# Later loads issued by SyncE instead of GpSimd, twelve closing steps on GpSimd, and a bf16 product at the end

## The chip, the cores and the metric

The kernel runs on one core of one Trainium2 chip. The metric is the device time of one execution in microseconds (us); less is better. A core has five engines with a queue of instructions each: PE (TensorE, matmuls), DVE (VectorE), ACT (ScalarE), POOL (GpSimd) and SP (SyncE, which here only issues transfers). Within an engine the instructions run in the order in which they were written; between engines they wait for each other by semaphores. Transfers, whichever engine issues them, run on 16 DMA engines.

## The reference

One transformer block on x of 2048 rows and D = 512 columns, in bf16:

```
mod = silu(c) @ w_mod                      # six vectors of 512: sa, ca, ga, sb, cb, gb
h = layernorm(x) * (1 + ca) + sa
q = h @ wq                                 # 32 heads of 128; 8 cached k/v heads of 2048 x 128
p = softmax(q k^T / sqrt(128));  x = x + ga * ((p v) @ wo)
h = layernorm(x) * (1 + cb) + sb
z = gelu(h @ w_in)                         # 2048 x 1792; z1, z2 its halves of 896
x = x + gb * ((z1 * (w_sp @ layernorm(z2) + b_sp)) @ w_out)
```

## The kernel before

The attention runs over 8 groups (one k/v head with its 4 query heads) and, within a group, over 16 tiles of 128 query rows: 128 units `u`, group `u // 16`, tile `u % 16`. A unit has 8 slots. In slot `i` PE makes 1024 columns of scores of unit `u` (`qk`), ACT takes their exponential, and PE does an eighth of the products with v of one or two earlier units (`pv`, `pv_rows`), four matmuls of the query projection of a later block (`qproj`), and in the last slots a head of the output projection of a still earlier unit (`wo_proj`). The order of the work is written out by hand: `at(unit, slot, fn)` puts a step in front of a slot, and `fill` puts one behind it. The instructions of each engine then stand in that order, as the tile framework's scheduler is switched off (`manual_schedule`); it still adds the semaphore waits.

A unit is computed in one of two ways. Most units from 8 to 118, two of every three, are "row units" (`by_rows`): scores have a query row to a partition, ACT sums each row while it takes the exponential (L1018), and SP then turns each head's 128 x 2048 block with a transposing transfer (`turn_rows`, L1050, 512 KB, four to a row unit), so that v can be the weights (L1065). The first row unit of a pair is multiplied with v two units later, the second three units later. The third unit of each triple, called a pause here, has transposed scores from the start (L1030, L1037) and needs no turn before v (L1086); only its small output is turned (L1109, `oT`). The rows wait in six buffers of 2048 columns, three of which are the space of `win_sb` and one that of `wmod_a`; the turned blocks go to `pT0`, `pT1` and `wsp`. The list `pauses` holds the second row unit of each pair, the one before a pause.

Each group needs its part of wq (512 KB, `load_wq`, L722), v (512 KB, `load_v`, L730, behind a memset of the column that sums the rows), wo (512 KB, `load_wo`, L740) and k (512 KB turned, `load_k`, L745). Groups 2 to 7 load them one at a time, each behind a different row pair, in slot 5 of the pause (wq, v, wo) or slot 1 (k). k is issued by SP, the queue of the row turns. wq, v and wo are issued by POOL, and in front of each stands `after_rows` (L1286): a copy of one element of the last turned block of that pair, for which POOL waits until that turn has landed. The later half of w_mod (2 MB into the space of `wsp`, L1257), group 1's loads (behind `after_pv`, L1290), w_in (1.75 MB, L1258), w_out and the b_sp rows (L1440, L1441) go through POOL as well. Transfers that SP issues use eight semaphores in turn; each waits for the landing of the one eight places before it.

`wo_proj` adds each head's product to the fp32 accumulator of its tile (`xacc`, L1130, L1136). In the last group the closing step of a tile follows on DVE: multiply by `ga_rows` (L1158), add x (L1159), and at once the statistics of the second layernorm (`ln_stats`, L698, L699). `ln2` does the rest one and two units later: the reciprocal root on POOL (L679, L683), the normalised tile on DVE (L687), its turn on SP (L1177, `xnT`), and the modulation on DVE (L1184).

The second half of the block follows: `z2_tile` (L1321), `z1_tile` (L1360), statistics and normalisation of z2 (L1343, L687), the spatial product with w_sp, whose turned blocks SP loads (`load_wsp`, L1216; `spatial`, L1486), and the last product with w_out (L1519). `finish_tile` multiplies by `gb_rows` into an fp32 `tmp` (L1531), adds x into `yout` (L1532) and stores it (L1533).

The lines that place the loads:

```
pauses = [u for u in row_units if not by_rows(u + 1)]
...
        last = next(u for u in pauses if u >= it + from_it and u > last)
        at(last + 1, 5, lambda u=last: after_rows(u))
        at(last + 1, 5, load)
    last = next(u for u in pauses if u >= it + 8 and u > last)
    at(last + 1, 1, lambda g=g: load_k(g))
```

Of the kernel before, what the change touches and what calls it, by code (L numbers as in the profile page):

```python
# [10 lines left out]
BF16 = mybir.dt.bfloat16  # L11
FP32 = mybir.dt.float32
ACT = mybir.ActivationFunctionType
ALU = mybir.AluOpType
AX = mybir.AxisListType
P = 128
# [559 lines left out]
def kernel(  # L576
# [19 lines left out]
    nc = tc.nc  # L596
    _, S, D = A_x.shape
    _, HKV, SK, DH = A_k_cache.shape
    HQ = A_wq.shape[1] // DH
    REP = HQ // HKV  # L600
    F = B_w_in.shape[1]
    FH = F // 2
    NMOD = w_mod.shape[1]
    assert DH == P and D == 512 and S % 512 == 0 and SK % 1024 == 0 and FH % P == 0 and REP == 4
    NT = S // P
    NDT = D // P
    NKT = SK // P
    NFT = FH // P
    NCH = S // 512
    CT = 512 // P  # L610
# [11 lines left out]
    v_dram = A_v_cache[0].rearrange("g (t p) d -> p g t d", p=P)  # L622
# [3 lines left out]
    wmod_dram = w_mod.rearrange("(p dt) n -> p dt n", p=P)  # L626
    c_dram = c[0].rearrange("(p j) -> p j", p=P)
    win_dram = B_w_in.rearrange("(dt p) f -> p dt f", p=P)
    wout_dram = B_w_out.rearrange("(ft p) d -> p ft d", p=P)
# [10 lines left out]
    stat = fast.enter_context(tc.tile_pool(name="stat", bufs=2))  # L640
# [7 lines left out]
    ga_rows = res.tile([P, D], FP32, name="ga_rows")  # L648
    gb_rows = res.tile([P, D], FP32, name="gb_rows")
    modc = res.tile([P, 6 * NDT], FP32, name="modc")  # L650
    rall = res.tile([P, NT * HQ], FP32, name="rall")
# [68 lines left out]
    def load_wq(g, engine):  # L720
        wqs[g] = early.tile([P, NDT, REP * DH], BF16, name="wq_g")
        engine.dma_start(  # L722
            out=wqs[g][:], in_=wq_dram[:, :, g * REP * DH : (g + 1) * REP * DH]
        )

    def load_v(g):
        v1 = late.tile([P, NKT, DV], BF16, name="v1")
        nc.gpsimd.memset(v1[:, :, DH:DV], 1.0)
        if g > 0:
            nc.gpsimd.dma_start(out=v1[:, :, 0:DH], in_=v_dram[:, g])  # L730
        else:
            nc.sync.dma_start(out=v1[:, 0 : NKT // 2, 0:DH], in_=v_rows)
            nc.sync.dma_start(
                out=v1[:, NKT // 2 : NKT, 0:DH], in_=v_dram[:, 0, NKT // 2 : NKT]
            )
        groups.setdefault(g, {})["v1"] = v1

    def load_wo(g, engine):
        wo_g = late.tile([P, REP, D], BF16, name="wo_g")
        engine.dma_start(out=wo_g[:], in_=wo_dram[:, g * REP : (g + 1) * REP, :])  # L740
        groups[g]["wo"] = wo_g

    def load_k(g):
        kT = early.tile([P, SK], BF16, name="kT")
        nc.sync.dma_start_transpose(out=kT[:], in_=A_k_cache[0, g])  # L745
        groups.setdefault(g, {})["kT"] = kT
# [218 lines left out]
    NU = HKV * NT  # L965
# [27 lines left out]
    def at(it, slot, fn):  # L993
        later.setdefault((it, slot), []).append(fn)
# [123 lines left out]
    def wo_proj(u):  # L1118
        g, j = divmod(u, NT)
        each = by_rows(u)  # L1120
        ps = {}

        def into(first, X_ps, scale):
            if first:
                xaccs[j] = late.tile([P, D], FP32, name=f"xacc{j}", bufs=1)
            xa = xaccs[j]
            if scale is None and first:
                nc.vector.tensor_copy(out=xa[:], in_=X_ps[:])
            elif scale is None:
                nc.vector.tensor_tensor(out=xa[:], in0=X_ps[:], in1=xa[:], op=ALU.add)  # L1130
            elif first:
                nc.vector.tensor_scalar(
                    out=xa[:], in0=X_ps[:], scalar1=scale, scalar2=None, op0=ALU.mult
                )
            else:
                nc.vector.scalar_tensor_tensor(  # L1136
                    out=xa[:], in0=X_ps[:], scalar=scale, in1=xa[:], op0=ALU.mult, op1=ALU.add
                )

        def mm(hh):  # L1140
            if hh == 0 or each:
                ps[0] = bank("misc")
            nc.tensor.matmul(  # L1143
                ps[0][:],
                lhsT=oTs[u][:, hh, :],
                rhs=groups[g]["wo"][:, hh, :],
                start=(hh == 0 or each),
                stop=(hh == REP - 1 or each),
            )
            if each:  # L1150
                c0 = u * REP + hh
                into(g == 0 and hh == 0, ps[0], rall[:, c0 : c0 + 1])
            elif hh == REP - 1:
                into(g == 0, ps[0], None)
            if hh < REP - 1 or g < HKV - 1:
                return
            xa = xaccs[j]
            nc.vector.tensor_tensor(out=xa[:], in0=xa[:], in1=ga_rows[:], op=ALU.mult)  # L1158
            nc.vector.tensor_tensor(  # L1159
                out=x_sb[:, j, :], in0=xa[:], in1=x_sb[:, j, :], op=ALU.add  # L1160
            )
            ln_stats(mv2, j, x_sb[:, j, :])

        return [lambda hh=hh: mm(hh) for hh in range(REP)]
# [89 lines left out]
    ln1_at(1, (0, 7), (1, 2), (2, 2))  # L1254
    ln1_at(2, (2, 4), (3, 1), (4, 5))
    ln1_at(3, (5, 1), (5, 5), (7, 4))
    at(2, 5, lambda: nc.gpsimd.dma_start(out=wmod_b, in_=wmod_dram[:, :, 2 * D : NMOD]))  # L1257
    at(NU - 2, 4, lambda: nc.gpsimd.dma_start(out=win_sb, in_=win_dram))  # L1258
    at(4, 4, mod_cols_b)
    at(5, 4, mod_rows)  # L1260

# [18 lines left out]
    at(NU + 1, 0, wsp0)  # L1280
    for st in range(NT):
        at(NU + 1 + st // 4, 2 * (st % 4), lambda st=st: load_wsp(wsp[0], 0, st))
    def after_rows(u):

        seen = stat.tile([1, 1], BF16, name="seen")
        nc.gpsimd.tensor_copy(out=seen[:], in_=pTs[u][0:1, NKT - 1, 511:512])  # L1286

    def after_pv(u):
        seen = stat.tile([1, 1], FP32, name="seen")
        nc.gpsimd.tensor_copy(out=seen[:], in_=rall[0:1, u * REP : u * REP + 1])  # L1290

    at(5, 0, lambda: after_pv(3))
    pauses = [u for u in row_units if not by_rows(u + 1)]
    for g in range(1, HKV):
        it = (g - 1) * NT
        loads = (
            (0, lambda g=g: load_wq(g, nc.gpsimd)),
            (4, lambda g=g: load_v(g)),
            (6, lambda g=g: load_wo(g, nc.gpsimd)),
        )  # L1300
        last = it - 1
        for from_it, load in loads:
            if g == 1:
                at(5, 0, load)
                continue
            last = next(u for u in pauses if u >= it + from_it and u > last)
            at(last + 1, 5, lambda u=last: after_rows(u))
            at(last + 1, 5, load)
        last = next(u for u in pauses if u >= it + 8 and u > last)
        at(last + 1, 1, lambda g=g: load_k(g))  # L1310


    zs = {}
# [90 lines left out]
    for it in range(NU + 6):  # L1404
        if it < NU:
            if it % CT == 0 and it // CT + 1 < NB:
                set_fill(it // CT + 1)
        elif it == NU:
            free_a.close()
            z2p = fast.enter_context(tc.tile_pool(name="z2p", bufs=1))  # L1410
            zs["z2"] = z2p.tile([P, NT, FH], BF16, name="z2")
        pvs = [u for u in range(max(it - 5, 0), min(it, NU)) if pv_at(u) == it]
        wos = [u for u in range(max(it - 8, 0), min(it, NU)) if wo_at(u) == it]
        wf = [fn for u in wos for fn in wo_proj(u)]
        for i in range(NSLOT):
            for fn in later.pop((it, i), []):
                fn()
            if it < NU:
                qk(it, i)
            if len(pvs) == 1:  # L1420
                pv_part(pvs[0], i, NSLOT)
            elif pvs:
                n = NSLOT // 2
                pv_part(pvs[i // n], i % n, n)
            for fn in fill.pop((it, i), []):
                fn()
            if i >= NSLOT - len(wf):
                wf[i - NSLOT + len(wf)]()
            if it >= NU:
                zrun(3)  # L1430
        for u in wos:
            if u >= (HKV - 1) * NT:
                ln2(it, u % NT)
        if it == NU + 2:
            free_b.close()
            mlp = fast.enter_context(tc.tile_pool(name="mlp", bufs=1, side="right"))
            zs["z1T"] = mlp.tile([P, NFT, S], BF16, name="z1T")
            wout_sb = mlp.tile([P, NFT, D], BF16, name="wout_sb")
            bsp_bc = mlp.tile([P, S], BF16, name="bsp_bc")
            nc.gpsimd.dma_start(out=wout_sb[:], in_=wout_dram)  # L1440
            nc.gpsimd.dma_start(out=bsp_bc[:], in_=B_b_sp.partition_broadcast(P))  # L1441
    assert not later and not fill
    for t in range(1, 3):
        wsp[t] = mlp.tile([P, NT, 512], BF16, name=f"wsp{t}")
# [81 lines left out]

    def finish_tile(t, jj, src):
        j = t * CT + jj
        tmp = mlp.tile([P, D], FP32, name="tmp", bufs=2)
        yout = mlp.tile([P, D], BF16, name="yout", bufs=2)  # L1530
        nc.vector.tensor_tensor(out=tmp[:], in0=src, in1=gb_rows[:], op=ALU.mult)  # L1531
        nc.vector.tensor_tensor(out=yout[:], in0=tmp[:], in1=x_sb[:, j, :], op=ALU.add)  # L1532
        nc.scalar.dma_start(out=out_dram[:, j, :], in_=yout[:])  # L1533
# [84 lines left out]
```

## Time and profile before

| | |
|---|---|
| time, median of 3 runs | 1322.26 us (1316.48 to 1336.3) |
| the profiled execution: its own time, its span | 1325.27 us, 1323.5 us |
| ACT, DVE, POOL busy | 84%, 52%, 4% of the span |
| POOL's transfers (queue q0) | 16.91 MB, 5.1% of 16 DMA engines |
| landing of wq, v, wo from POOL (median) | 4.3, 7.1, 8.4 us |
| row turn `wsp<-win_sb` (median) | 5.5 us |
| yout, 16 additions | 11.1 us, 692 ns each |

The page gives for each engine the time in which it was busy. A group of instructions has its line in the code, engine, operation, result and operands, count, busy time, the mean of one, and the idle time of the engine before them with what ended it. A line "A <- B: 3.3, 2, 2.5" in the list of waits says that A's engine waited for B for 3.3 us in two waits, the longest 2.5. In lines in order of time the first number is the start in us from the span's start, the second the duration; "SPq" is an issue by SP's queue, and the time given is that of issuing, not of the transfer. "Landing" is counted from the issue. PEclk is the clock that PE was granted, as a share of the full one. The DMA share counts overlapping pieces of work on an engine, and so can be over 1.

### The profile page before, as it was taken

How to read it: one execution, taken by the hardware profiler on the slowest of the kernel's cores; microseconds unless marked ns; L12 is line 12 of the kernel's file. 1: busy time of each engine (PE TensorE's matmuls, PEld its weight loads, DVE VectorE, ACT ScalarE, POOL GpSimd, SP SyncE). 2: the span in 40 equal slices, each digit the busy share in tenths (PEclk: the TensorE clock that was granted, in tenths of full speed). 3: DMA queues.
4: the chain of work that ended last, by engine and by line, in shares of the span. 5: the costliest groups of instructions: out<-in, count | busy, mean ns of one | idle time of the engine just before them, and what ended most of it. 6: DMA issues, size and time to landing. Idle time of an engine off the chain costs nothing.

```text
span 1323.5 us, 22994 instructions
## 1 busy us (share of the span) xinstructions
PE 1303.0 (98%) x8807; PEld 705.4 (53%) x8807; DVE 690.9 (52%) x1754; ACT 1113.2 (84%) x1653; POOL 55.1 (4%) x116
## 2 busy tenths in 40 slices
PE   9999999999999999999999999999999999999998
PEld 5664555555445555555445555555555566644445
DVE  6533445545445454445444555454545678794444
ACT  7899999999899999999989999999999988751000
POOL 1200000000000000000000000000000001120000
PEclk9999999999999999999999999999999999999999
DMA  7779999999999999999999999999999911464300
GB/s 180 152 102 195 166 187 174 188 182 182 151 185 179 183 178 180 182 173 182 174 159 192 182 180 187 185 181 176 169 202 179 167 27 29 110 139 100 72 21 31
DMA packets 724358, 203.86 MB, mean 154 GB/s; under 512 B 713904, under 2 KB 720304, under 8 KB 724240
## 3 DMA queue, kind: packets, MB, share of 16 engines
q1 hardware_dynamic: 717216, 183.17, 79.2%
q0 software_dynamic: 4432, 16.91, 5.1%
q10 hardware_dynamic: 2592, 2.23, 0.5%
q8 instruction: 71, 1.16, 0.4%
q14 instruction: 47, 0.39, 0.1%
HBM read 21.89 MB, written 2.10 MB: 18 GB/s over the span
## 4 chain that ended last, share of the span: by engine, by line
PE 93%; DMA 5%; DVE 1%; ACT 0%; issue 0%; POOL 0%; ACTq 0%; DVEq 0%
PE o_ps L1065 18%; PE s_ps L1011 18%; PE o_ps L1086 14%; PE s_ps L1030 13%; PE misc L1143 8%; PE misc L947 8%; PE misc L1486 7%; DMA wsp<-win_sb 2%; PE s_ps L1321 2%; PE s_ps L1360 2%; PE o_ps L1519 1%; DMA wsp<-in_w_mod_dram 1%; DMA wsp<-pn 1%; PE s_ps L1519 0%; ACT win_sb L1018 0%; DMA wsp<-wmod_a 0%
## 5 line engine op out<-in xcount | busy, mean ns | idle before, releaser
L1037 ACT ACTIVATE pT<-s_ps 128x1024 bf16<-128x1024 f32 x408 | 413.2, 1025 | 40.2 <-PE s_ps L1030 23.0
L1011 PE MATMUL s_ps<-kT,qT 128*128 128x512 bf16 x1184 | 352.7, 379 | 2.4 <-ACT win_sb L1018 2.4
L1018 ACT ACTIVATE win_sb<-s_ps 128x1024 bf16<-128x1024 f32 x298 | 304.7, 1023 | 6.2 <-DMA wsp<-win_sb 2.7
L1086 PEld LDWEIGHTS <-pT 128*128 128x128 bf16 x3264 | 218.5, 98 | 95.9
L1030 PE MATMUL s_ps<-qT,kT 128*128 128x512 bf16 x864 | 256.7, 379 | 0.4 <-ACT pT L1037 0.2
L1086 PE MATMUL o_ps<-v,pT 128*128 128x129 bf16 x3264 | 251.6, 220 | 0.0
L1136 DVE SCALAR_TENSOR_TENSOR xacc<-misc,rall,xacc 128x512 f32<-128x512 f32 x290 | 217.0, 748 | 55.4 <-PE misc L1143 49.3
L1018 ACT ACTIVATE pn<-s_ps 128x1024 bf16<-128x1024 f32 x196 | 200.5, 1023 | 1.7 <-PE s_ps L1011 0.4
L1143 PE MATMUL misc<-wo_g,oT 128*128 128x512 bf16 x512 | 194.5, 380 | 1.6 <-DVE xacc L1136 1.6
L1065 PEld LDWEIGHTS <-v 128*128 128x128 bf16 x1184 | 115.5, 98 | 149.2 <-issue 9.1
L947 PE MATMUL misc<-hT,wq_g 128*128 128x512 bf16 (+2 forms) x520 | 187.0, 371 | 0.1
L1065 PE MATMUL o_ps<-wsp,v 128*128 128x512 bf16 x592 | 176.1, 379 | 7.4 <-DMA wsp<-pn 3.3
L1065 PE MATMUL o_ps<-pT,v 128*128 128x512 bf16 x592 | 176.3, 381 | 0.0
L1011 PEld LDWEIGHTS <-qT 128*128 128x128 bf16 x1184 | 115.8, 98 | 107.9 <-issue 4.7
L958 DVE CAST qT<-misc 128x512 bf16<-128x512 f32 x125 | 85.8, 687 | 162.6 <-PE misc L947 162.6
L1054 DVE TENSOR_TENSOR tot<-rs 128x1 f32<-128x1 f32 x296 | 45.5, 154 | 168.7 <-ACT win_sb L1018 114.7
L1030 PEld LDWEIGHTS <-kT 128*128 128x128 bf16 x864 | 83.5, 98 | 88.4 <-issue 4.8
L1018 ACT ACTIVATE wmod_a<-s_ps 128x1024 bf16<-128x1024 f32 x98 | 100.2, 1024 | 1.0 <-PE s_ps L1011 1.0
L1486 PE MATMUL misc<-wsp,z 128*128 128x512 bf16 (+2 forms) x560 | 100.7, 336 | 0.0
L1097 DVE RECIPROCAL rall<-o_ps 128x2 f32<-128x2 f32 x108 | 18.3, 170 | 117.8 <-PE o_ps L1086 114.4
L1486 PEld LDWEIGHTS <-z 128*128 128x128 bf16 x560 | 50.6, 98 | 48.7 <-issue 0.2
L947 PEld LDWEIGHTS <-wq_g 128*128 128x128 bf16 x528 | 50.4, 98 | 37.3 <-issue 0.4
(112 smaller groups left out, 809.7 us busy)
## 6 DMA issues: line engine op xcount, KB each, us to landing
wq_g<-in_A_wq_dram POOLq DMA_DIRECT2D x7, 512.0 KB, 4.3
v<-in_A_v_cache_dram POOLq DMA_DIRECT2D x7, 512.0 KB, 7.1
wo_g<-in_A_wo_dram POOLq DMA_DIRECT2D x7, 512.0 KB, 8.4
wsp<-in_w_mod_dram POOLq DMA_DIRECT2D x1, 2048.0 KB, 11.8
out_dram<-yout ACTq DMA_DIRECT2D x16, 128.0 KB, 1.7
win_sb<-in_B_w_in_dram POOLq DMA_DIRECT2D x1, 1792.0 KB, 8.0
x_sb<-in_A_x_dram SPq DMA_DIRECT2D x3, 512.0 KB, 8.0
wsp<-win_sb SPq DMA_TRANSPOSE x75, 5.5
```

Source lines behind the costliest of these rows:

```text
L947: nc.tensor.matmul(ps[0][:, o0 : o0 + n], lhsT=wqs[g][:, dt, hh * DH : (hh + 1) * DH], rhs=hTs[ch][:, dt, c0 : c0 + n], start=(dt == 0), s ...
L958: nc.vector.tensor_copy(out=dst, in_=src)
L1011: nc.tensor.matmul(s_ps[:, c * 512 : (c + 1) * 512], lhsT=qTs[b][:, hh, jj * P : (jj + 1) * P], rhs=groups[g]["kT"][:, k0 : k0 + 512], sta ...
L1018: nc.scalar.activation(out=rows_of(u, hh)[:, half * HK : (half + 1) * HK], in_=s_ps[:], func=ACT.Exp, scale=inv_sqrt_dh, accum_out=rsums[u ...
L1030: nc.tensor.matmul(s_ps[:, h * 512 : (h + 1) * 512].rearrange("p (r q) -> p r q", r=REP), lhsT=groups[g]["kT"][:, kt * P : (kt + 1) * P], ...
L1037: nc.scalar.activation(out=pTs[u][:, 2 * i : 2 * i + 2, :], in_=s_ps[:].rearrange("p (k q) -> p k q", k=2), func=ACT.Exp, scale=inv_sqrt_dh,)
L1054: nc.vector.tensor_tensor(out=tot[:], in0=rs[:, 2 * hh : 2 * hh + 1], in1=rs[:, 2 * hh + 1 : 2 * hh + 2], op=ALU.add)
L1065: nc.tensor.matmul(o_pss[u][:], lhsT=groups[g]["v1"][:, kt, 0:DH], rhs=pTs[u][:, kt, :], start=(kt == 0), stop=(kt == NKT - 1),)
L1086: nc.tensor.matmul(o_ps[:, hh % 2, 0 : DH + 1], lhsT=pTs[u][:, kt, hh * P : (hh + 1) * P], rhs=groups[g]["v1"][:, kt, 0 : DH + 1], start=( ...
L1136: nc.vector.scalar_tensor_tensor(out=xa[:], in0=X_ps[:], scalar=scale, in1=xa[:], op0=ALU.mult, op1=ALU.add)
L1143: nc.tensor.matmul(ps[0][:], lhsT=oTs[u][:, hh, :], rhs=groups[g]["wo"][:, hh, :], start=(hh == 0 or each), stop=(hh == REP - 1 or each),)
L1486: nc.tensor.matmul(g_pss[f][:, :n], lhsT=z2[:, st, f * P : (f + 1) * P], rhs=wsp[t][:, st, c0 : c0 + n], start=(st == 0), stop=(st == NT - ...
```

## The change

All loads that POOL issued go to SP. `load_v` takes SP for every group, `load_wq` and `load_wo` are called with SP, and `after_rows` and `after_pv` are dropped. The loads of groups 2 to 7 now stand in slot 1 of the pause, directly behind the last row turn of the pair (which is issued in slot 0), as k's did. Group 1's three loads move from (5,0) to (6,2), w_mod's from (2,5) to (1,4), w_in's from unit 126 to slot 2 of unit 120 (`TURN_B` is 119); those of w_out and b_sp keep their place in the program.

For the tiles j < NT - CT (0 to 11 of 16) POOL does the two closing operations; the statistics stay on DVE. In `finish_tile` the product with gb is written as bf16 into the same space, and so the addition reads two bf16 operands.

```
-            nc.gpsimd.dma_start(out=v1[:, :, 0:DH], in_=v_dram[:, g])
+            nc.sync.dma_start(out=v1[:, :, 0:DH], in_=v_dram[:, g])
...
-            nc.vector.tensor_tensor(out=xa[:], in0=xa[:], in1=ga_rows[:], op=ALU.mult)
-            nc.vector.tensor_tensor(
+            engine = nc.gpsimd if j < NT - CT else nc.vector
+            engine.tensor_tensor(out=xa[:], in0=xa[:], in1=ga_rows[:], op=ALU.mult)
+            engine.tensor_tensor(
                 out=x_sb[:, j, :], in0=xa[:], in1=x_sb[:, j, :], op=ALU.add
             )
             ln_stats(mv2, j, x_sb[:, j, :])
...
-    at(2, 5, lambda: nc.gpsimd.dma_start(out=wmod_b, in_=wmod_dram[:, :, 2 * D : NMOD]))
-    at(NU - 2, 4, lambda: nc.gpsimd.dma_start(out=win_sb, in_=win_dram))
+    at(1, 4, lambda: nc.sync.dma_start(out=wmod_b, in_=wmod_dram[:, :, 2 * D : NMOD]))
+    at(TURN_B + 1, 2, lambda: nc.sync.dma_start(out=win_sb, in_=win_dram))
...
-    at(5, 0, lambda: after_pv(3))
...
-            (0, lambda g=g: load_wq(g, nc.gpsimd)),
+            (0, lambda g=g: load_wq(g, nc.sync)),
             (4, lambda g=g: load_v(g)),
-            (6, lambda g=g: load_wo(g, nc.gpsimd)),
+            (6, lambda g=g: load_wo(g, nc.sync)),
+            (8, lambda g=g: load_k(g)),
         )
...
-            if g == 1:
-                at(5, 0, load)
+            if g == 1 and from_it < 8:
+                at(6, 2, load)
                 continue
             last = next(u for u in pauses if u >= it + from_it and u > last)
-            at(last + 1, 5, lambda u=last: after_rows(u))
-            at(last + 1, 5, load)
-        last = next(u for u in pauses if u >= it + 8 and u > last)
-        at(last + 1, 1, lambda g=g: load_k(g))
+            at(last + 1, 1, load)
...
-            nc.gpsimd.dma_start(out=wout_sb[:], in_=wout_dram)
-            nc.gpsimd.dma_start(out=bsp_bc[:], in_=B_b_sp.partition_broadcast(P))
+            nc.sync.dma_start(out=wout_sb[:], in_=wout_dram)
+            nc.sync.dma_start(out=bsp_bc[:], in_=B_b_sp.partition_broadcast(P))
...
-        tmp = mlp.tile([P, D], FP32, name="tmp", bufs=2)
+        tmp = mlp.tile([P, D], FP32, name="tmp", bufs=2)[:].bitcast(BF16)[:, 0:D]
```

More of the change, by code (lines that the diff above doesn't have):

```diff
@@ L1282 @@
         at(NU + 1 + st // 4, 2 * (st % 4), lambda st=st: load_wsp(wsp[0], 0, st))
[L1283 to L1290, printed above, removed]
-    at(5, 0, lambda: after_pv(3))
     pauses = [u for u in row_units if not by_rows(u + 1)]
```

## The prediction, on record before the change was run

> **What bounds the kernel now.** I read the page first (busy shares, clock, queues), then the list of PE's waits, then the busy time of PE in stretches behind each kind of load, then single instructions where a stretch was not full.
>
> ```profile
> span 1323.5 us, 22994 instructions
> ...
> PE 1303.0 (98%) x8807; PEld 705.4 (53%) x8807; DVE 690.9 (52%) x1754; ACT 1113.2 (84%) x1653; POOL 55.1 (4%) x116
> ...
> q1 hardware_dynamic: 717216, 183.17, 79.2%
> ```
>
> PE is busy for 1303.0 of 1323.5 us: no edit that leaves the matmuls alone can gain more than 20.5 us of idle time, plus what PE loses at a lowered clock. So 2% (26 us, about what a measurement of this kernel can tell from no change) cannot be won. The question is which pieces of those 20.5 us go, and whether new ones come. The second scarce thing is the DMA engines: SyncE's queue q1, with the row turns, holds them 79% of the span.
>
> The next lines are sums over stretches of 23 us that begin at a load in the row stage: the seven k-cache loads, which SyncE issues already (sum 161), then two of the six v loads that Pool issues, and the sums of the six v loads, the six wo loads and the six wq loads. The second column is PE's busy time, the column behind POOL's the granted clock.
>
> ```profile
> core 0: us, PE busy (x) PEld busy (x) DVE busy (x) ACT busy (x) POOL busy (x), PEclk, DMA share, GB/s
> ...
> sum 161.00, PE 161.00 PEld 85.91 DVE 73.00 ACT 158.72 POOL 0.00; mean PE 23.00 PEld 12.27 DVE 10.43 ACT 22.67 POOL 0.00
> ...
> 344.00:367.00 23.00, 19.89 (x120) 9.95 (x119) 8.90 (x28) 17.70 (x33) 0.91 (x1) 0.93 1.07 141
> ...
> 639.00:662.00 23.00, 21.33 (x129) 10.80 (x128) 10.37 (x29) 20.73 (x35) 1.07 (x1) 1.00 1.06 182
> ...
> sum 138.00, PE 132.97 PEld 68.75 DVE 62.36 ACT 128.81 POOL 6.50; mean PE 22.16 PEld 11.46 DVE 10.39 ACT 21.47 POOL 1.08
> ...
> sum 138.00, PE 133.22 PEld 67.50 DVE 67.51 ACT 129.90 POOL 4.12; mean PE 22.20 PEld 11.25 DVE 11.25 ACT 21.65 POOL 0.69
> ...
> sum 138.00, PE 138.00 PEld 72.77 DVE 64.67 ACT 136.18 POOL 4.55; mean PE 23.00 PEld 12.13 DVE 10.78 ACT 22.70 POOL 0.76
> ```
>
> See: behind a k load from SyncE PE is never idle; behind v loads from Pool it loses 138 - 132.97 = 5.03 us, behind wo 4.78, behind wq nothing. That is nearly all that the row stage loses. How it happens shows at 344 us:
>
> ```profile
> 343.75 1.16 POOL L730 DMA_DIRECT2D v<-in_A_v_cache_dram  x1 [0.19 <-issue]
> ...
> 344.16 3.63 SPq L1050 DMA_TRANSPOSE wsp<-win_sb  x1
> 347.84 9.33 SPq L1050 DMA_TRANSPOSE wsp<-wmod_a  x1
> ...
> 358.98 0.69 PE L1011 MATMUL s_ps<-kT,qT 128*128 128x512 bf16 x2 [2.24 <-ACT win_sb L1018]
> 359.46 1.06 PE L1065 MATMUL o_ps<-pT,v 128*128 128x512 bf16 x2
> ```
>
> Pool waits for the last turn of a row pair, and so issues its load when the next pair's first turn is issued as well. The two run together: the turn of 344.16 lands after 13.55 us (median 4.8 to 5.5), SyncE needs 9.33 us to issue the next, ACT finds its row buffer taken, PE idles 2.24 us and then runs at half clock for some 3.5 us (1.06 for 0.59).
>
> **The change part by part.** The sum is made against the profiled execution: 1325.27 us, its span 1323.5 and 1.8 around it. That is 3.0 above the median of 1322.26.
>
> *18 loads of the row stage (groups 2 to 7), to SyncE.* Each stands right behind the last turn of a row pair, the place that the k load has now: one unit (some 8.7 us) before the next turn, which then follows it instead of running beside it. Each adds one issue to SyncE: 0.5 to 0.6 us by its wq, wo and x loads at the start; the v half of the same pattern (L733) took 2.08, so a whole v up to 4.2; the k load takes 2.5 (1.9 to 3.5). SyncE has room, it waits for ACT some 690 us in all. Behind it stand only the turns. Removed: 5.03 + 4.78 = 9.8 us, and at a clock of 0.93 over 23 us another 1.6. New waits: from below 0 (the seven k loads, of the same 512 KB), from above what PE's waits for late turns are now, 0.8 to 2.5 us each. I take 0, the k load being the same queue, place and size. -11.4.
>
> *The modulation load (2 MB) from slot (2,5) on Pool to (1,4) on SyncE, group 1's loads to (6,2).* Now PE waits for it at 48.97 us; in the stretch of 30 to 60 us it is busy 29.15 of 30. Issued at some 29 us instead of 37.07, with the same 11.8 us to land, it is there 8 us early: -0.85. Behind it on SyncE are two oT turns, some 10 us later; their matmuls come at 50.7 us, and they land by 42. Group 1's loads move to a stretch (60 to 85 us) with a DMA share of 0.43. 0.
>
> *w_in from unit 126 to 120, w_out and b_sp on SyncE.* SyncE's queue is then nearly empty; an xnT turn behind w_in waits at most w_in's 8.0 us, and its reader comes 9 slots (10 us) later. w_out waits for the last closing step (5.8 us on Pool now), in front of three w_sp turns and the last xnT turn. That turn slips from 1169.14 by some 3 us (w_out and b_sp take 1.0 and 0.6 to issue, three turns 4.1). PE is full from 1166 to 1196 us; the normalised last chunk, ready at 1195.7, is first read after 24 matmuls, at about 1200.6. That cover, 4.9 us, hides it; without it the cost would be 3 us. 0.
>
> *The closing steps of 12 tiles on Pool.* Two DVE instructions leave, but the bn_stats behind them must now wait on DVE for Pool, and behind it the reciprocals, the qT casts and the xacc updates that free PE's banks.
>
> ```profile
> 1079.97 0.69 DVE L1158 TENSOR_TENSOR xacc<-xacc,ga_rows 128x512 f32<-128x512 f32 x1
> 1080.70 0.69 DVE L1159 TENSOR_TENSOR x_sb<-xacc,x_sb 128x512 bf16<-128x512 f32 x1
> 1081.42 0.69 DVE L698 BATCH_NORM_STATS2 bnst<-x_sb 128x6 f32<-128x512 bf16 x1
> ...
> PE misc L1143 <- DVE xacc L1136: 1.6, 1, 1.6
> ...
> L728 POOL MEMSET v<- 128x128 bf16 x8 | 1.6, 200 | 0.3 <-PE s_ps L1011 0.3
> ...
> L679 POOL TENSOR_SCALAR ve_lnz<-mvz 128x4 f32<-128x4 f32 x4 | 1.1, 264 | 17.9 <-DVE mvz L1344 17.9
> ...
> masks.py:199 POOL TENSOR_SCALAR_AFFINE_SELECT ident<-ident 128x128 bf16<-128x128 bf16 x1 | 0.3, 292 | 0.1
> ```
>
> No row shows a 128x512 operation on Pool. From below: the memset, 200 ns for 128 columns and 101 for 4, gives 0.8 ns a column, 0.5 us. From above: tensor_scalar, 232 ns for one column and 264 for four, 10.7 ns a column, 5.7 us. Nearest in width and kind is the affine select: (292 - 101) / 124 = 1.5 ns a column, 0.9 us with one input; with two I take 1.25 us. bn_stats starts now 1.45 us after the last xacc update (two of 0.69 and gaps); then 2 x 1.25 + 0.2 of handing over (0.09 us from DVE to Pool, 0.09 within Pool, 0.03 back) = 2.7: DVE is 1.25 us later. From there I went down DVE's queue behind each of the 12 steps, as far as its idle time lasts, to the matmuls that wait for it. The margins: none at 1098.3 us (PE already waits 1.6 there), 0.45 at 1080.7, 0.9 at 1042.3, 1.3 and more elsewhere: 1.25 + 0.8 + 0.35 = 2.4. At 0.5 us a step nothing is lost (0.2 won); at 5.7 us DVE is 10 us late twelve times, 96 us. +2.4.
>
> The Trainium skill, GPSIMD Engine Reference, section Performance versus the Vector engine, speaks against this edit: a two-input elementwise operation takes Pool 1.96 times as long as DVE. By that, an estimate, 1.36 us a step and +3.4 in place of +2.4; no run here shows it yet.
>
> *bf16 product with gb.* yout (L1532, 0.69 us) becomes all bf16 like yT (L1514, 0.42 to 0.43 at 128x512). Only the last of 16 is on the path: -0.27. If the narrower operands bring nothing: 0.
>
> Sum: 1325.27 - 11.4 - 0.85 + 2.4 - 0.27 = 1315.1 us.
>
> **The rivals.** *The loads hold up the turns* (slower). The turn behind a load must now wait for all of it. For: the queues are full (79% of 16 engines over the whole span), the v load is 2048 pieces of 256 B, and the first turns of a pair land with little to spare (at 123.7 us for a matmul at 123.8). Against: the k loads. If each of the 18 cost 1.6 us (the typical wait for a turn now), 28.8 us come back: 1344. It decides from 10 / 18 = 0.6 us a load.
>
> *The waits stay.* The bytes are the same and the engines the same 16; the DMA share is 1.06 and 1.07 in the two v stretches above. If lost engine time and not the meeting of two queues makes the turns late, only -0.85, +2.4 and -0.27 remain: 1326.5. Against: wq loads from Pool and k loads cost nothing, at shares up to 1.19. The Trainium skill, DMA: Bandwidth & Descriptors, section Issuing engines are not separate DMA queues, is on this rival's side: the engine that issues saves only issue time. The k stretches above speak against it.
>
> *A slow Pool.* Above 2.1 us a step the delay passes 3 us, costs 12 us, and eats the gain; at 2.5 us (3.8 late) it is some 20: 1333. At 3.2 us it reaches 1349, 2% slower. For: tensor_scalar's slope. Against: memset and affine select.
>
> **How the numbers follow.** Forecast 0.65, by itself 1310 to 1322 (all waits gone and Pool at 0.5 us gives 1312.5, two more for the spread of runs; Pool at 1.9 us gives 1322). Waits stay 0.15. Turns held up 0.10. Slow Pool 0.10, a third of it below 1329. So 1310 to 1329 leaves out 0.17. Faster by over 2%: 0.01, as PE's busy time alone is over that bound. Slower by over 2%: 0.06, from the upper parts of the slow Pool and of the turns held up (2 us and more a load). Within: 0.93.
>
> **What would show it.** Right: PE full in the 23 us behind each wq, v and wo load; no PE wait on a transposed tile; no turn landing after 9 us or more; L857 without a wait; Pool tensor_tensor rows at 1 to 1.5 us; PE waits on xacc of 2 to 5 us between 1040 and 1130. Wrong: SyncE issues of v over 5 us with PE waits behind them; turns that land late with no other load in flight; Pool rows over 2 us; z2 statistics waiting for the last xnT turn and PE idle near 1200 us.

## The result, and the profile after

The changed kernel takes 1314.0 us (median of 13 runs, 1312.99 to 1314.83), the kernel before 1321.69 us in the runs beside it (13 runs, 1316.48 to 1336.3). The ratio is 0.9935, 95% interval 0.9913 to 0.9957 (it leaves out slow runs and is not the quotient of the two medians, 0.9942): a gain of some 8 us that is well above its own uncertainty and well below 2%. The prediction was 1315.1. The runs also lie far closer together: 1.8 us from lowest to highest, where before it was 20 (ten more runs of the changed kernel, e0 below, span 6.7).

The profiled execution of the changed kernel took 1312.99 us, 12.3 less than that of the kernel before (1325.27). That is more than the 7.7 us between the medians: the one was the shortest of its 13 runs, the other 3.6 us above the median of the runs before. What follows accounts for these two executions. This is the page of the changed kernel's, in part:

```profile
span 1311.2 us, 22903 instructions
...
PE 1300.0 (99%) x8807; PEld 705.3 (54%) x8807; DVE 667.6 (51%) x1730; ACT 1112.1 (85%) x1653; POOL 58.9 (4%) x96
...
q1 hardware_dynamic: 741168, 199.55, 83.6%
...
q0 software_dynamic: 224, 0.53, 0.2%
```

PE's idle time fell from 20.5 to 11.2 us and its busy time by 3.0. The transfers of POOL's queue q0 are gone but for 0.53 MB, the two rows ga and gb of the modulation, which POOL still loads; SP's q1 holds the DMA engines 83.6% of the span, 79.2% before.

The next lines are the sums over 23 us behind each load again: one of the six v loads and their sum, then the sums of the six wo and the six wq loads, all from SP now.

```profile
339.00:362.00 23.00, 23.00 (x156) 12.42 (x154) 11.49 (x32) 22.67 (x38) 0.00 (x0) 1.00 1.00 189
...
sum 138.00, PE 138.00 PEld 74.47 DVE 68.29 ACT 135.96 POOL 0.00; mean PE 23.00 PEld 12.41 DVE 11.38 ACT 22.66 POOL 0.00
...
sum 138.00, PE 138.00 PEld 74.34 DVE 69.28 ACT 135.96 POOL 0.00; mean PE 23.00 PEld 12.39 DVE 11.55 ACT 22.66 POOL 0.00
...
sum 138.00, PE 138.00 PEld 74.50 DVE 70.73 ACT 135.75 POOL 0.41; mean PE 23.00 PEld 12.42 DVE 11.79 ACT 22.62 POOL 0.07
```

PE is full behind all 18 loads, at a clock of 1.00. SP's queue around one of them, the v load of group 3 (start, time of issuing):

```profile
339.05 0.78 SPq L730 DMA_DIRECT2D v<-in_A_v_cache_dram  x1
343.67 1.76 SPq L1050 DMA_TRANSPOSE wsp<-win_sb  x1
345.88 2.35 SPq L1050 DMA_TRANSPOSE wsp<-wmod_a  x1
```

The load takes 0.78 us to issue and has 4.6 us to run before the next turn is issued; v loads land 4.7 us after their issue (median of seven), so the load is only just out of the way. Before, the same two turns took 3.63 and 9.33 us to issue. Of the row turns whose landing is on record (223 of 296, 186 before) none takes more than 7.2 us to land, where it was up to 13.55. These are the landings of all row turns, before and after:

```profile
DMA to landing us min/median/max: 4.3/4.9/13.5
```

```profile
DMA to landing us min/median/max: 4.3/4.7/7.2
```

PE's waits of the changed kernel:

```profile
PE misc L1143 <- DVE xacc L1136: 2.7, 1, 2.7
...
PE s_ps L1030 <- ACT pT L1037: 1.2, 2, 0.9
PE misc L857 <- DMA wmod_a<-in_w_mod_dram: 0.3, 1, 0.3
```

There is no wait for a turned block (L1065) or for a row buffer (L1011). Two lines are worse than before: L1143, 1.6 before, is the closing steps; L1030 is a wait of 0.93 us at 72.65 us that was not there.

Where the 12.3 us of the two profiled executions come from, by stretches of the span (idle time of PE, or busy time in the second line):

| | before | after | change | forecast |
|---|---|---|---|---|
| idle 85 to 1060 us, the row stage | 9.88 | 0.05 | -9.8 | -9.8 |
| PE busy, whole span | 1303.0 | 1300.0 | -3.0 | -1.6 |
| idle 30 to 60 us, w_mod | 0.85 | 0.00 | -0.85 | -0.85 |
| idle 60 to 85 us, group 1's loads | 0.00 | 0.93 | +0.93 | 0 |
| idle 1060 to 1135 us, closing steps | 1.56 | 2.68 | +1.1 | +2.4 |
| idle 1280 us to the end | 6.13 | 5.47 | -0.66 | -0.27 |
| idle 0 to 30 us | 2.12 | 2.03 | -0.1 | 0 |

### The profile page after: what moved, and what is told of

It is laid out like the page before. It is cut to its first block, busy times and chain, and to the rows that moved or that the text cites. A ratio compares the mean times of both kernels' runs of the same rounds, so it can differ in the third digit from the quotient of the medians.

```text
span 1311.2 us, 22903 instructions
## 1 busy us (share of the span) xinstructions
PE 1300.0 (99%) x8807; PEld 705.3 (54%) x8807; DVE 667.6 (51%) x1730; ACT 1112.1 (85%) x1653; POOL 58.9 (4%) x96
## 3 DMA queue, kind: packets, MB, share of 16 engines
q1 hardware_dynamic: 741168, 199.55, 83.6%
q8 instruction: 71, 1.16, 0.4%
## 4 chain that ended last, share of the span: by engine, by line
PE 98%; DVE 1%; DMA 0%; ACT 0%; POOL 0%; issue 0%; SPq 0%; ACTq 0%; DVEq 0%
PE s_ps L1011 20%; PE o_ps L1065 19%; PE o_ps L1086 15%; PE s_ps L1030 14%; PE misc L1143 8%; PE misc L947 8%; PE misc L1475 7%; PE s_ps L1310 2%; PE s_ps L1349 2%; PE o_ps L1508 1%; DMA wmod_a<-in_w_mod_dram 0%; PE s_ps L1508 0%; ACT win_sb L1018 0%; PE misc L857 0%; ACT pT L1037 0%; DVE hT L816 0%
## 5 line engine op out<-in xcount | busy, mean ns | idle before, releaser
L1011 PE MATMUL s_ps<-kT,qT 128*128 128x512 bf16 x1184 | 352.1, 379 | 0.0
L1030 PE MATMUL s_ps<-qT,kT 128*128 128x512 bf16 x864 | 256.7, 379 | 1.3 <-ACT pT L1037 1.2
L1136 DVE SCALAR_TENSOR_TENSOR xacc<-misc,rall,xacc 128x512 f32<-128x512 f32 x290 | 216.9, 748 | 54.8 <-PE misc L1143 48.5
L1143 PE MATMUL misc<-wo_g,oT 128*128 128x512 bf16 x512 | 194.0, 379 | 2.7 <-DVE xacc L1136 2.7
L1065 PEld LDWEIGHTS <-v 128*128 128x128 bf16 x1184 | 115.8, 98 | 139.8 <-issue 0.4
L1065 PE MATMUL o_ps<-wsp,v 128*128 128x512 bf16 x592 | 176.1, 379 | 0.0
L1065 PE MATMUL o_ps<-pT,v 128*128 128x512 bf16 x592 | 175.4, 379 | 0.0
L1011 PEld LDWEIGHTS <-qT 128*128 128x128 bf16 x1184 | 115.7, 98 | 104.8 <-issue 1.2
L1030 PEld LDWEIGHTS <-kT 128*128 128x128 bf16 x864 | 83.4, 98 | 90.4 <-issue 6.6
```

Of the source, the lines that this page charges most:

```text
L1011: nc.tensor.matmul(s_ps[:, c * 512 : (c + 1) * 512], lhsT=qTs[b][:, hh, jj * P : (jj + 1) * P], rhs=groups[g]["kT"][:, k0 : k0 + 512], sta ...
L1030: nc.tensor.matmul(s_ps[:, h * 512 : (h + 1) * 512].rearrange("p (r q) -> p r q", r=REP), lhsT=groups[g]["kT"][:, kt * P : (kt + 1) * P], ...
L1065: nc.tensor.matmul(o_pss[u][:], lhsT=groups[g]["v1"][:, kt, 0:DH], rhs=pTs[u][:, kt, :], start=(kt == 0), stop=(kt == NKT - 1),)
L1136: nc.vector.scalar_tensor_tensor(out=xa[:], in0=X_ps[:], scalar=scale, in1=xa[:], op0=ALU.mult, op1=ALU.add)
L1143: nc.tensor.matmul(ps[0][:], lhsT=oTs[u][:, hh, :], rhs=groups[g]["wo"][:, hh, :], start=(hh == 0 or each), stop=(hh == REP - 1 or each),)
```

## The experiments

Twelve kernels ran in three sets; those of a set ran on the same chip, and so their times are compared within a set first. The theory: a load that GpSimd issues while the first turn of a row pair runs makes that turn late, as the two queues share the DMA engines, and SyncE's order removes the meeting. The rivals: only the time of the load matters; only the queue; and for the closing steps, that GpSimd's part costs more, or less, than the one tile.

### The queue or the time of the load (e3, e4)

The change moved the 18 loads of groups 2 to 7 in two ways at once: to another queue, and to an earlier time. The two kernels do one each. In e3 GpSimd issues them again, behind a copy of one element of the pair's last row, so that they start beside the last turns of the pair and not behind them (its kernel has two lines more in front, so L1052 below is L1050):

```
+    def after_exp(u):
+        seen = stat.tile([1, 1], BF16, name="seen")
+        nc.gpsimd.tensor_copy(out=seen[:], in_=rows_of(u, REP - 1)[0:1, SK - 1 : SK])
...
+            if from_it < 8:
+                at(last + 1, 1, lambda u=last: after_exp(u))
             at(last + 1, 1, load)
```

> The 18 loads of groups 2 to 7 go back to GpSimd, but start when the exponential of the pair's last row is done, that is when the pair's last turn is issued, as early as in the changed kernel. If what counts is the time (the load must not run beside the first turns of the next pair), no PE wait comes back and the time stays at 1314. If what counts is the queue (a load beside turns of another queue always delays them), the last turn of the pair is late, and waits of the old size come back: up to 1325.

In e4 SyncE issues them late, behind the first turn of the next pair:

```
-            at(last + 1, 1, load)
+            if from_it < 8:
+                at(last + 2, 3, load)
+            else:
+                at(last + 1, 1, load)
```

> The 18 loads stay with SyncE, but stand behind the first turn of the next pair, the time at which they ran before. If what counts is the time, PE waits as before behind v and wo and the time is about 1325. If what counts is the queue, the turns are only shifted by the load's own 2.5 us or so and the time is 1314 to 1318.

e3 took 1315.17 us (12 runs, ratio to the kernel before 0.9933, 0.9911 to 0.9954), e4 1317.1 us (12 runs, 0.9937, 0.9916 to 0.9958). On the same chip e2 (below), whose loads and closing wait are those of the changed kernel, took 1314.49. So neither half, taken back by itself, brings the old waits of 9.8 us back: the old time with the new queue costs about 2.6 us by the medians, the old queue at the new time 0.7, which the ranges of the runs (1313.12 to 1321.05 and 1312.67 to 1317.69) do not tell from nothing.

What each does to the turns shows in SP's queue. Of e3, with the load of GpSimd at 334.36 us and the last two turns of that pair:

```profile
334.36 1.16 POOL L730 DMA_DIRECT2D v<-in_A_v_cache_dram  x1 [0.25 <-issue]
```

```profile
335.31 7.37 SPq L1052 DMA_TRANSPOSE pT<-win_sb  x2
344.45 3.03 SPq L1052 DMA_TRANSPOSE wsp<-win_sb  x1
```

The turns beside the load are late in e3 as well: 14 of the 224 whose landing is on record took over 7.5 us, up to 9.3, none in the changed kernel. But they are the last turns of a pair, which the products with v need some 8 us or more after they land (in the changed kernel), and the next pair's first turn at 344.45 us finds the load gone. PE's waits on turned blocks stay at none. In e4 no turn takes more than 7.5 us, but the ones behind the load, at 5.5 to 7.5 us instead of 4.8, are those without slack, and a few of them are waited for:

```profile
PE o_ps L1065 <- issue: 0.6, 2, 0.4
PE o_ps L1065 <- DMA wsp<-pn: 0.5, 1, 0.5
...
PE o_ps L1065 <- DMA wsp<-wmod_a: 0.3, 1, 0.3
```

That is 1.4 of the 3.9 us between the profiled executions of e4 and e2 (2.6 by the medians). The rest has its place at 73 us, before any load that was moved: PE's wait on ACT is 2.2 us there (1.3 in e2), and the granted clock from 60 to 85 us is 0.93 (1.00 in e2). So the waits of the kernel before came only with both, the other queue and the place beside the turns without slack. This bears out the theory in its mechanism and corrects it: it was enough to take away either of the two.

Two things stay open. The delay on one turn was up to 8.7 us in the kernel before and 4.5 in e3, from the same queue; what the place adds to it is not shown. And the six wq loads of the kernel before met the same turns from the same queue and cost nothing. They landed 4.0 to 4.4 us after their issue, v and wo 6.0 to 11.1; no run here varies what makes that difference.

The Trainium skill, DMA: Bandwidth & Descriptors, section Issuing engines are not separate DMA queues, says that transfers of all issuing engines interleave on the same 16 DMA engines, and that issuing from several saves only issue time. PE's time in e3 agrees: at the same place the other queue cost the row stage nothing. The turns do not quite: with the loads at the same place, the latest one landed after 9.3 us in e3 and after 7.2 us in the changed kernel.

### The closing steps (e1, e2, e5)

Three kernels around the two closing steps of 12 tiles. e1 leaves them on VectorE:

```
-            engine = nc.gpsimd if j < NT - CT else nc.vector
+            engine = nc.vector
```

> All 16 closing steps stay on VectorE; the rest is the changed kernel (1314.0 us). If the price is what the forecast says (2.4 us on three tiles), the time falls to 1311.6. If only the tile without margin pays, as the trace of the changed kernel reads (PE's wait on xacc 2.7 us there for 1.6 before), it falls by 1.1 to 1312.9 and that wait is 1.6 again. If the two steps on GpSimd cost nothing, 1314.0.

e1 took 1312.3 us (6 runs, 1311.76 to 1313.36; 0.9909, 0.9875 to 0.9943), 2.2 less than e2 on the same chip. Its wait is that of the kernel before again:

```profile
PE misc L1143 <- DVE xacc L1136: 1.6, 1, 1.6
```

So the step to GpSimd cost 1.1 us by the trace and 1.7 to 2.2 by the medians (the changed kernel's, from another chip, and e2's): between the two prices that were expected, with the trace on the side of the lower one. How it costs is in the changed kernel's rows for GpSimd (count, busy time, mean ns), then in the tile without margin:

```profile
L1159 POOL TENSOR_TENSOR xacc<-xacc,ga_rows 128x512 f32<-128x512 f32 x12 | 15.2, 1267 | 217.4 <-DVE xacc L1130 187.3 <-DVE xacc L1136 30.0
L1160 POOL TENSOR_TENSOR x_sb<-xacc,x_sb 128x512 bf16<-128x512 f32 x12 | 13.9, 1154 | 0.9
```

```profile
1084.75 1.27 POOL L1159 TENSOR_TENSOR xacc<-xacc,ga_rows 128x512 f32<-128x512 f32 x1 [3.93 <-DVE xacc L1130]
...
1086.09 1.15 POOL L1160 TENSOR_TENSOR x_sb<-xacc,x_sb 128x512 bf16<-128x512 f32 x1
1087.28 0.69 DVE L698 BATCH_NORM_STATS2 bnst<-x_sb 128x6 f32<-128x512 bf16 x1 [2.61 <-POOL x_sb L1160]
...
1088.11 0.72 DVE L1136 SCALAR_TENSOR_TENSOR xacc<-misc,rall,xacc 128x512 f32<-128x512 f32 x1
...
1088.88 0.38 PE L1143 MATMUL misc<-wo_g,oT 128*128 128x512 bf16 x1 [2.68 <-DVE xacc L1136]
```

VectorE has nothing to do for 2.61 us, with the xacc update queued behind its wait that frees the bank PE needs: work was taken off VectorE, and yet it is later, as the next thing in its queue needs GpSimd's result. e2 and e5 keep GpSimd and move the statistics away from behind it. e2:

```
-            ln_stats(mv2, j, x_sb[:, j, :])
+            if j >= NT - CT:
+                ln_stats(mv2, j, x_sb[:, j, :])
...
+        if j < NT - CT:
+            at(it + 1, 0, lambda: ln_stats(mv2, j, x_sb[:, j, :]))
         at(it + 1, 0, first)
```

> The closing steps of 12 tiles stay on GpSimd, but their statistics go to the start of the next unit, so that VectorE does not wait for GpSimd. If VectorE's wait of 2.6 us behind each step is what PE pays at the tile without margin, PE's wait on xacc of 2.7 us goes and the time is about 1311.3, below the kernel with the steps on VectorE. Rival: the statistics are only late somewhere else, in front of the reciprocals and xacc updates of the next unit, and the time stays at 1313 to 1314.

e2 took 1314.49 us (11 runs, 0.993, 0.9905 to 0.9955): nothing won. Its lines at the same tile say why:

```profile
1088.47 0.69 DVE L698 BATCH_NORM_STATS2 bnst<-x_sb 128x6 f32<-128x512 bf16 x1 [2.60 <-POOL x_sb L1160]
...
1090.08 0.38 PE L1143 MATMUL misc<-wo_g,oT 128*128 128x512 bf16 x1 [2.67 <-DVE xacc L1136]
```

A tile is closed in the last slot of its unit, so the start of the next unit is the same place in VectorE's queue: the edit moved nothing. e5 moves the statistics three slots on:

```
+        if j < NT - CT:
+            at(it + 1, 3, lambda: ln_stats(mv2, j, x_sb[:, j, :]))
+            at(it + 1, 3, first)
+            at(it + 1, 5, second)
+        else:
             at(it + 1, 0, first)
             at(it + 1, 4, second)
```

> As e2, but the statistics of the 12 tiles stand in slot 3 of the next unit, some 3 us behind the last xacc update, by which time GpSimd's two steps (2.4 us) are done; the normalised tile moves from slot 4 to 5. If VectorE's wait for GpSimd is the price of the steps, it is below 0.5 us each now, PE's wait on xacc of 2.7 us goes and the time is 2 to 2.7 us below the changed kernel. Rival: the later turn of the normalised tile delays the last tiles, and nothing is won.

e5 took 1311.63 us (7 runs, 1310.91 to 1312.51; 0.9909, 0.9873 to 0.9945), the unaltered changed kernel on the same chip (e0, below) 1314.93. Its PE waits:

```profile
PE s_ps L1030 <- ACT pT L1037: 1.4, 2, 1.2
...
PE misc L1143 <- DVE qT L958: 0.6, 1, 0.6
```

The wait of 2.7 us is gone but for 0.6 on another instruction, as expected: 2.1 us by the trace, 3.3 by the medians. That the steps on GpSimd are then a gain over VectorE, and not only cheaper than before, e10 and e11 have to show (below).

### The start of the row stage (e0, e6, e7, e8, e9)

The changed kernel once more:

> The changed kernel once more, unaltered, beside the next three: 1314 us, with PE's wait on xacc of 2.7 us in the stretch of the closing steps and a gap on ACT of 1.7 to 3.0 us near 70 us, where group 1's three loads are in flight.

It took 1314.93 us (10 runs, 1312.98 to 1319.64; 0.9919, 0.9889 to 0.9949). The profiled execution was the longest of these, 1319.64, and shows a wait that the first profile of this kernel did not have. SP's queue and GpSimd's, at the first turn of unit 8:

```profile
68.20 9.02 SPq L740 DMA_DIRECT2D wo_g<-in_A_wo_dram  x1
...
84.73 13.39 SPq L1050 DMA_TRANSPOSE wsp<-win_sb  x3
```

```profile
86.15 0.55 POOL L1214 DMA_DIRECT2D gb_rows<-mod  x1 [12.68 <-DMA mod<-modc]
```

```profile
PE o_ps L1065 <- DMA wsp<-wmod_a: 2.7, 1, 2.7
```

Group 1's three loads, issued at 67 to 68 us, land 10.3, 14.5 and 20.8 us later; wo's 9.02 us of issuing hold SP's queue. The first row turn lands after 11.9 us (5.8 in the first profile). Two loads run beside it: wo of group 1, which lands at 89.0 us (at 85.1, before the turn, in the first profile), and gb's rows, the last load that GpSimd still issues. PE waits 2.7 us. In the first profile this stretch had 1.0 us to spare, and what was costed at nothing, group 1's loads, sits in front of it. e6 spreads them:

```
-                at(6, 2, load)
+                at(*{0: (6, 2), 4: (7, 2), 6: (7, 6)}[from_it], load)
```

> Group 1's three loads no longer stand together in slot (6,2) but at (6,2), (7,2) and (7,6), 512 KB each. If the crowding of the DMA engines by the three makes ACT's gap near 70 us, the gap goes and the time falls by 0.9 to 2.2 us, to about 1312.5. If the gap comes from something else at that place in the program, it stays and the time is 1314.

e6 took 1318.36 us (12 runs, 0.9947, 0.9923 to 0.9971), 3.4 more than e0: the wrong direction. v is in flight when the first turn starts at 88 us, PE waits 0.9 us at 88, 0.8 at 102 and 1.1 at 128 us, and the gap near 70 us stays, with only wq of the three in flight:

```profile
72.49 11.53 ACT L1037 ACTIVATE pT<-s_ps 128x1024 bf16<-128x1024 f32 x11 [2.36 <-PE s_ps L1030]
```

e7 is e5 and e6 together:

> e5 and e6 together. If both gains are there and don't touch each other, the time is their sum below the changed kernel: 1310 to 1311 us.

It took 1315.09 us (11 runs, 0.9934, 0.9908 to 0.996): the statistics' gain and e6's loss add up (e7 is 3.5 us above e5, as e6 is 3.4 above e0). So the loads have to go the other way, early. e8 is e5 with

```
-                at(6, 2, load)
+                at(3, 4, load)
```

> e5 (1311.6 us) with group 1's three loads at (3,4) in place of (6,2), some 22 us earlier, in the stretch from 30 to 60 us where the DMA engines are 44% busy. If those loads make ACT's gap near 70 us (1.9 us in e5, 1.2 of it a wait of PE), the gap is below 0.5 us and the time about 1310.5, and the first row turns land with more to spare, so that the spread of the runs narrows. If the gap belongs to that place in the program, whatever is in flight, the time stays at 1311.6.

e8 took 1309.5 us (6 runs, 1309.24 to 1310.0; 0.9908, 0.9878 to 0.9938), the fastest of all. It ran on another chip than e5, so its gain over e5 rests on the trace: wo's issue by SP, and the stretch from 60 to 85 us, where e5's PE was busy for 23.82 us:

```profile
45.56 2.49 SPq L740 DMA_DIRECT2D wo_g<-in_A_wo_dram  x1
```

```profile
60.00:85.00 25.00, 25.00 (x256) 17.13 (x254) 8.64 (x25) 23.45 (x27) 2.87 (x4) 1.00 0.48 51
```

PE is full, the DMA share is 0.48 (0.99 in the changed kernel, 0.43 before), and all six runs are within 0.8 us. e9, like e8 an edit of e5, instead takes away the other suspect, the row loads on GpSimd:

```
-            nc.gpsimd.dma_start(out=rows[:], in_=line[:].partition_broadcast(P))
+            at(13 + 3 * i, 1, lambda rows=rows, line=line: nc.sync.dma_start(
+                out=rows[:], in_=line[:].partition_broadcast(P)))
```

> e5 with the two row loads of the modulation (ga, gb, 256 KB each), the last that GpSimd issues, moved to SyncE behind the row pairs of units 11 and 14. If gb's load from GpSimd beside the first row turn is what makes that turn late (6 to 12 us, with a margin of 0.1 to 0.9), the turn lands within 5 us and the slowest runs come down to the median; the median itself falls by 0 to 0.5. If the crowd of group 1's loads alone makes it late, nothing changes.

e9 took 1310.21 us (6 runs, 1309.52 to 1311.12; 0.9913, 0.9883 to 0.9943). The first turn lands after 5.2 us with group 1's loads still at (6,2), its margin grows to 1.6 us, and the gap near 70 us stays (PE waits 0.8 us). So gb's rows add a little to the lateness of the first turn (5.2 us without them, 5.7 in e8 and 6.1 in e5 with them), and group 1's loads bring the wait at 72 us, which e8 on the same chip does not have: two causes. The 11.9 us of e0 are not shown to be either's alone; e7, whose v load was still in flight at its first turn, has 8.8. Nor is it shown that the spread of the runs comes from this stretch: the runs of e8 and e9 lie within 0.8 and 1.6 us and those of e0 within 6.7, but the seven of e5, with both suspects in place, lie within 1.6 as well.

### All together, and GpSimd's part again (e10, e11)

> e8 and e9 together: about 1310 us, if both touch different waits; no turn later than 7.5 us and no wait of PE between 60 and 110 us.

> e10 with the closing steps of the 12 tiles on VectorE again; the statistics stay in slot 3 of the next unit. If GpSimd's part is what helps, 1 us or so slower than e10 (VectorE has two more steps of 0.69 us in front of the xacc updates); if the later place of the statistics alone took PE's wait away, the same as e10 within 0.5 us.

e10 joins the edits of e8 and e9, and e11 is e10 with e1's line. e10 took 1310.58 us (6 runs, 1309.22 to 1311.02; 0.9915, 0.9885 to 0.9945), no better than e8 or e9. PE has no wait between 60 and 110 us and no turn on record takes over 6.9 us, as expected, but with group 1's loads early the first turns had 1.0 us to spare already. e11 took 1312.56 us (8 runs, 1311.58 to 1313.34; 0.9931, 0.9907 to 0.9955), 2.0 more than e10. The stretch of the closing steps in e10, then in e11:

```profile
1060.00:1100.00 40.00, 39.43 (x402) 26.98 (x401) 28.41 (x71) 34.29 (x34) 16.13 (x20) 1.00 0.15 32
```

```profile
1060.00:1100.00 40.00, 38.79 (x394) 26.39 (x392) 33.58 (x81) 33.40 (x34) 3.92 (x10) 1.00 0.16 38
```

VectorE is busy 5.2 us more of 40, and PE loses 0.64. The two profiled executions lie 2.5 us apart; of the rest, 0.3 is a wait near 70 us, 0.3 lies in the first 30 us and 1.2 in PE's idle time from 1280 us on, and the trace does not tie these to the edit. GpSimd's part helps with the statistics out of its way, by 0.6 us in the trace and 2.0 by the medians.

## Why the prediction was right, point by point

**The loads to SyncE (-11.4).** Right in place and size: 9.8 us of waits went, none came, SyncE's issue of v took 0.8 us at the load shown where up to 4.2 was allowed for, and the turns behind the loads are not held up. One reading was wrong and did no harm: the next turn was to follow one unit (8.7 us) behind the load, but at the v load of group 3 it followed 4.6 us behind it. The k load of the kernel before had shown that: it is issued at 263.80 us, the next turn at 267.03. The clock was taken at 1.6 us, and that fits: the granted clock is 0.93 in the 23 us behind the 344 us stall, 1.00 behind the other v and wo loads, and 1.00 there after the change. PE's busy time fell by 3.0; the other 1.4 is not the clock, and what it is stays open. As to the reason, the prediction had the meeting of the two queues as the cause. e3 and e4 show that it was harmful only at the turns without slack: GpSimd's queue at a better time would have done nearly as well (e3), and SyncE's queue at the old time would have cost 1.4 us of waits in place of 9.8 (e4).

**w_mod early (-0.85).** Right: PE is full from 30 to 60 us.

**Group 1's loads (0).** This step failed. It read the share of 0.43 in the stretch from 60 to 85 us as room, but not what lies at its end: the loads, issued together, keep the DMA engines at a share of 0.99 until the first row turn (the column in front of the last).

```profile
60.00:85.00 25.00, 24.07 (x245) 16.35 (x243) 8.48 (x23) 22.06 (x23) 2.82 (x4) 1.00 0.99 108
```

And this is what ACT and PE do in that stretch:

```profile
71.58 9.33 ACT L1037 ACTIVATE pT<-s_ps 128x1024 bf16<-128x1024 f32 x9 [1.66 <-PE s_ps L1030]
72.65 0.59 PE L1030 MATMUL s_ps<-qT,kT 128*128 128x512 bf16 x2 [0.93 <-ACT pT L1037]
```

ACT starts 1.66 us late on scores that PE had finished at 69.95, so something other than PE held it; PE then waits 0.93 us for ACT. With the three loads gone from there (e8) PE's wait falls to 0.2. The cost was 0.9 us in the first profile; in the longest run of e0 PE's waits from 60 to 120 us come to 4.7 us, with gb's rows beside the first turn.

**w_in, w_out, b_sp (0).** Right: PE is full from 1135 to 1280 us.

**The closing steps (+2.4).** The mechanism was right, the size was 1.1. The duration fits, 1.27 and 1.15 us for 1.25, and so does the delay, 2.61 us of waiting for 1.45 of work before, 1.16 later. The Trainium skill, GPSIMD Engine Reference, section Performance versus the Vector engine, has Pool take 1.96 times VectorE's time for an fp32 addition of 2048 columns; here, at 512 columns, it was 1.83 and 1.67 times (1267 and 1154 ns by 692), so the price by that page, +3.4, was further off than +2.4. What failed is the margin of 0.45 us at the second tile, and likewise 0.9 at the third. Before, VectorE had itself waited for PE behind the statistics of the second tile:

```profile
1081.42 0.69 DVE L698 BATCH_NORM_STATS2 bnst<-x_sb 128x6 f32<-128x512 bf16 x1
...
1083.05 0.17 DVE L1097 RECIPROCAL rall<-o_ps 128x2 f32<-128x2 f32 x1 [0.72 <-PE o_ps L1086]
...
1083.60 0.68 DVE L958 CAST qT<-misc 128x512 bf16<-128x512 f32 x1
```

and in the changed kernel, at the same tile:

```profile
1069.73 0.69 DVE L698 BATCH_NORM_STATS2 bnst<-x_sb 128x6 f32<-128x512 bf16 x1 [2.61 <-POOL x_sb L1160]
...
1070.56 0.14 DVE L1097 RECIPROCAL rall<-o_ps 128x2 f32<-128x2 f32 x1
...
1071.07 0.68 DVE L958 CAST qT<-misc 128x512 bf16<-128x512 f32 x1
```

From the statistics to the qT cast it was 2.18 us and is 1.34: VectorE's own idle time of 0.72 takes most of the delay up, and 0.3 us is left by the cast, less than the margin. At the third tile, from the tile's last xacc update (L1130) to the next unit's first (L1136), it was 5.19 us and is 5.82: 0.6 us is left, less than the margin of 0.9.

**The bf16 product (-0.27).** Right: 425 ns an addition for 692.

```profile
L1521 DVE TENSOR_TENSOR yout<-tmp,x_sb 128x512 bf16<-128x512 bf16 x16 | 6.8, 425 | 0.7
```

The idle time at the end fell by 0.4 more, which nothing here explains.

**The sum.** The forecast of 1315.1 and the profile's 1312.99 differ by 2.1: the closing steps 1.3 too dear, 1.4 of PE's busy time not forecast, the end 0.4 and the start 0.1 too little, against 0.9 for group 1's loads. That the errors partly cancel is luck; the large term, 9.8 us of waits, was right by itself. Its size belongs to the one execution that was read: by the medians the change gained 7.7 us where 10.1 was forecast, and that the forecast still lies within 1.1 us of the median of 1314.0 owes something to having started 3.6 us above the median before. Of the rivals, turns held up by loads did not come (that rival needed 0.6 us a load); the waits did not stay; GpSimd was not slow (that rival needed 2.1 us a step).

## What to carry to other kernels

Before a load is moved, find which of the transfers around it have slack to their reader, and put it beside those: the same 512 KB cost nothing beside the last turns of a pair, from either queue, and up to 3.1 us of PE's time (in the 23 us from 344 us) beside the first ones of the next, from GpSimd's. A step given to a second engine saves nothing while the first engine's next instruction reads its result; move that reader behind work that doesn't need it (here three slots, -2.1 us by the trace, -3.3 by the medians), and only then is the move a gain. And a low DMA share over a stretch is no room if what follows directly behind it has no slack.

## What was not expected of the hardware

Behind 115 us, beside a 512 KB load of GpSimd's queue, a row turn took up to 13.55 us to land (9.3 in e3); in the runs whose loads all come from its own queue it took at most 7.9 (e9; 7.5 in e4). The median is 4.7 to 4.9. At the start of the row stage, with loads of both queues in flight, it was up to 11.9 (e0).

ACT stood still for 1.45 to 2.96 us near 70 us in the profiles of the changed kernel, e0 to e7 and e9, all with loads of group 1 in flight, and for 1.01 us or less in e8, e10 and e11, without them. PE had long delivered what ACT is said to wait for. That the gap is smaller without the loads is shown; what ACT waited for is not in the trace and stays open.
